# Moving fetches, stores, last sums and value products in a top-k attention and MLP kernel

## The chip, the cores and the metric

The kernel runs on one NeuronCore of a Trainium2 chip. A core has a matrix engine (PE, whose weight loads the profile lists apart as PEld), a vector engine (DVE), a scalar engine (ACT), a general engine (POOL) and a sync engine (SP). Each works through its own list of instructions, and semaphores tie them together. Nearly all DMAs of this kernel are issued by SP. The metric is the time of one execution on the device in microseconds (us); less is better.

## The reference

The inputs are `q`, `k`, `v` of shape 8 x 8 x 576 x 64 (batch, heads, sequence, head size), a gain of 512 and two weight matrices of 512 x 2048 and 2048 x 512. Attention keeps the 32 largest scores of each row, and an MLP with layer norm and a residual follows:

```python
scores = scale * np.matmul(q, k.transpose(0, 1, 3, 2))
kth = np.partition(scores, -32, axis=-1)[..., -32:-31]
scores = np.where(scores >= kth, scores, -1e9)
attn = np.exp(scores - scores.max(-1, keepdims=True))
attn = attn / (attn.sum(-1, keepdims=True) + 1e-9)
x = np.matmul(attn, v)                      # then heads side by side: 8 x 576 x 512
xn = (x - mean) / np.sqrt(var + 1e-6) * g_ln
out = x + np.maximum(xn @ w_ch1, 0.0) @ w_ch2
```

## The kernel before

**Units, jobs, groups.** A job is a pair of heads of one batch with some blocks of 128 queries; a unit is one query block of a job (both heads), or the last 64 rows of the sequence for both heads together (a rest unit). There are 160 units in 68 jobs of one to three units; the units of a job form a group. For each pair of heads the first job is fresh: `k` and `q` are loaded from the input (`load`, L316), turned by DVE (`turn_heads`, L343), and the turned `k` and late part of `q` are kept in DRAM (`keep_heads`, L357). Later jobs of the same pair are twins and read what was kept (`fetch_heads`, L364). The turned tiles (`kT`, `late_qT`) have two buffers each.

**The loop.** One loop runs over 166 steps, and the order in which it gives out instructions is the order on every engine. In step n: PE makes the scores of unit n+2 (unit n+1 up to step 16) in `scores` (L413), and ACT copies them out of PSUM (L394). DVE searches the 32nd largest value of unit n in four parts (`select`, L449 to L463) and starts unit n+1 (`halve`, L434), with POOL making the smaller halves (`lo`, L439 and L442). ACT masks unit n-1 (L490) and takes the exponentials of unit n-2 (L500). The exponentials of unit n-2 are turned to get keys on partitions, by PE and ACT copies (`turn`) or, for units that are not the last of their group in later batches, by DVE and two rounds of DMA (`move`, L532, L537, L540). The group that ended with unit n-3 gets its value products, 18 matmuls into `av` (`values`, L608 and L615), which ACT copies to `oT` (L620); PE turns them (L647) and ACT scales them into rows `x` (`place`, L624).

**Fill.** The MLP works on blocks of two row tiles. Its matmuls (`hidden` L748, `project` L905) wait in a list, and `fill`, called eight times a step, puts some of them between the other work, as many as a plan by costs allows. Each call advances a counter, `tick`. After the first block the projection uses seven products instead of eight: POOL makes sums of the hidden values (`sums` L835 to L837, `last_sum` L841), and differences of weights are made once in four steps (`form_pair`, L958 to L961), stored in DRAM (L963) and fetched for each block (L970).

**Later.** Work that needs not be done at once is held by `Later` lists and given out when it is old enough: `sums_later.settle(SUM_AGE)` with 7 ticks, once a step behind `halve` (L1226); `ends_later` with 6 ticks at each `fill`. A block's end is its scaling (ACT, L726), its residual (POOL, L721) and the stores of its rows (SP, L723). The residual puts the stores on a list, `stores`, and the next step's start sends them. `close` runs what is left of the previous block's ends when a block's projection begins.

**Plans.** `fetches` says in which step a twin's kept heads are fetched: `step = min(before.first, made - 1)`, where `made` is the step in which the job's first scores are made and `before.first` the first unit of the job before it. `fetch_heads` is called behind `halve` and `settle` of that step (L1229). The value products are called at L1213, behind two `fill`s. PSUM has five buffers for scores, turned tiles and `av`, and three for the MLP's products.

Of the kernel before, what the change touches and what calls it, by code (L numbers as in the profile page):

```python
# [29 lines left out]
def kernel(  # L30
# [41 lines left out]
    nc = tc.nc  # L72
# [174 lines left out]


    todo = []
    stores = []  # L250
    share = [0.0]
    owed = [0.0]

# [9 lines left out]
    tick = [0]  # L263

    class Later:
# [2 lines left out]
        def __init__(self):  # L268
            self.waiting = []

        def add(self, run):
            left = [run]

            def once():
                if left:
                    left.pop()()

            self.waiting.append((tick[0], once))
            return once

        def settle(self, age):
# [2 lines left out]
            for _, run in due_now:  # L284
                run()

    sums_later, ends_later = Later(), Later()

    def fill(least=0):
        tick[0] += 1  # L290
# [312 lines left out]
    def values(g):  # L603
        vb = g.job.v
        av = brief("av")
        for c in range(J):
            for h in range(2):
                nc.tensor.matmul(  # L608
                    av[h * D : (h + 1) * D, 0 : g.nq],
                    vb[:, h * J + c, :],  # L610
                    g.blocks[:, h, 0 : g.nq // 32, c, :],
                    start=(c == 0),
                    stop=False,
                )
        nc.tensor.matmul(  # L615
            av[:, 0 : g.nq], g.job.ends[:], g.pt[:, 2 * J, 0 : g.nq],
            start=False, stop=True,
        )
        g.oT = otpool.tile([P, GQ], FP32, tag="oT", name="oT")
        nc.scalar.copy(g.oT[:, 0 : g.nq], av[:, 0 : g.nq])  # L620

    def put(dst, ps, c0, den, d0):
        for h in range(2):
# [35 lines left out]
    class Block:  # L659
# [57 lines left out]
        def finish(self, i):  # L717
            o = self.o[i]

            def residual():  # L720
                nc.gpsimd.tensor_tensor(o[:], o[:], self.x[i], ALU.add)  # L721
                for dst, rows in self.dsts[i]:
                    stores.append(lambda d=dst, s=o[rows, :]: nc.sync.dma_start(d, s))  # L723

            def scaled():
                nc.scalar.activation(  # L726
                    o[:], o[:], AF.Identity,
                    bias=self.mv[:, i, 0:1], scale=self.rstd[:, i : i + 1],
                )
                self.ends.append(sums_later.add(residual))  # L730

            self.ends.append(ends_later.add(scaled))
# [83 lines left out]
        def seven(self):  # L816
# [47 lines left out]
            def evacuate(k):  # L864
# [4 lines left out]
                if k in home:  # L869
                    nc.scalar.copy(quarter(*home[k]), src)  # L870
                    if k == 1:
                        for j in range(G):
                            waiting[j]()
                            waiting[j] = sums_later.add(lambda j=j: last_sum(j))
                    return
                if k == 6:
                    joined[2]()
# [53 lines left out]
            )  # L931

    PER_ROW = 1.71e-3
    SUM_AGE, END_AGE, FETCH_AGE = 7, 6, 10
    blocks = []
    plain_done, formed, used, fetched = [None], [None], [], [0]

# [9 lines left out]
    def form_pair(i):  # L947

        lo, hi = slice(2 * i, 2 * i + 2), slice(NF // 2 + 2 * i, NF // 2 + 2 * i + 2)
        b11, b12 = w2[:, lo, 0 : 2 * P], w2[:, lo, 2 * P : DM]
        b21, b22 = w2[:, hi, 0 : 2 * P], w2[:, hi, 2 * P : DM]
        tt = nc.gpsimd.tensor_tensor
        x = xpool.tile([P, 2, DM], FP32, tag="x", name="form")
        t1, t2 = wt[:, 0, lo], wt[:, 1, lo]
        t4, t3 = (x[:, s].rearrange("p (f n) -> p f n", f=2) for s in range(2))
        tt(t1, b12, b11, ALU.subtract)  # L958
        tt(t2, b22, t1, ALU.subtract)
        tt(t3, t2, b11, ALU.subtract)  # L960
        tt(t4, b21, t2, ALU.subtract)  # L961
        for s in range(2):
            nc.sync.dma_start(scratch[:, s, i], x[:, s])  # L963
        if i == 3:
            formed[0] = now[0]
# [122 lines left out]
    for j in jobs[1:]:  # L1088
# [1 line left out]
        made = next(n for n in range(N) if units[j.first] in due(n))  # L1090
        step = min(before.first, made - 1)
        if j.twin:
            fetches.setdefault(step, []).append(j)
        else:
            turns[step] = j
            keeps[step + 1] = j
# [44 lines left out]
        return max(0.0, even) / SLOTS  # L1141

    recips, rows_of = {}, {}
    pairs_left = list(range(4))

    def arrived(n, key, x):
        blk, i = block_of[key]
# [18 lines left out]
    for n in range(END):  # L1166
# [16 lines left out]
        quick = ex.group if last and ex.group.quick else None  # L1183

        moved = ex is not None and ex.moved
        sent, stores[:] = stores[:], []

        if ex and not early:
            weigh(ex, 0)
        for x in due(n):  # L1190
            scores(x)
        if u:
            select(u, 0)
        for store in sent:
            store()
        if n in keeps:
            keep_heads(keeps[n])
        if n == gives_first:
# [12 lines left out]
            weigh(ex, 1)  # L1211
        fill()
        if g:  # L1213
            values(g)
        if parts and not moved:
            parts[0]()
        if ex and ex.rest:
# [8 lines left out]
        sums_later.settle(SUM_AGE)  # L1226
        for den in recips.pop(n, []):
            nc.vector.reciprocal(den, den)
        for j in fetches.get(n, []):  # L1229
            fetch_heads(j)  # L1230
        if n in turns:
            turn_heads(turns[n])
            later = fresh.index(turns[n]) + 1
# [37 lines left out]
        if quick:  # L1271

            values(quick)
            for den in recips.pop(n + 1):
                nc.vector.reciprocal(den, den)
            place(quick)
# [8 lines left out]
        for x in (g, quick):  # L1285
            if x and x.job.hp == NHP - 1:
                for qt in x.qts:
                    if qt < J:
                        arrived(n, (x.job.b, qt), xs[x.job.b, qt])
        if plain_done[0] is not None and plain_done[0] < n and len(pairs_left):  # L1290
            form_pair(pairs_left.pop(0))
        if late and late.job.hp == NHP - 1:
            r = late.job.b // 2
            if r % 2:
                for x in (r - 1, r):
                    arrived(n, ("r", x), rs[x])
        fill()
    while todo or stores or sums_later.waiting or ends_later.waiting:
        for store in stores:
            store()  # L1300
        stores.clear()
        tick[0] += 1
        ends_later.settle(1)
        sums_later.settle(1)
        fetch_forms(1)
# [33 lines left out]
```

## Time and profile before

| What | us |
|---|---|
| median of 3 runs | 1657.49 |
| range of the runs | 1655.69 to 1658.88 |
| the profiled execution | 1654.96 |
| its span, first to last instruction | 1653.2 |
| PE, DVE, ACT, POOL busy in it | 1513.9, 1459.4, 1069.8, 963.5 |
| PE's granted clock, mean | 0.968 |
| DVE's idle time at its costliest waits: scores' copies, exponentials' turns, row statistics | 14.8, 25.5, 21.8 |

The profile is of one execution. It lists busy time by engine and by groups of like instructions, who waited for whom, the chain of work that ended last, and the instructions in order of time. In a line such as `PE scps L413 <- DMA late_qT<-kept` the engine, the tile it writes and the line of code wait for what stands on the right. A line of the timeline gives start, duration, engine, line, operation, tiles (out<-in), shapes and count, and in brackets the idle time before it and what ended it. `PEld` is the weight load, `SPq` an issue on SP.

### The profile page before, as it was taken

The page shows a single profiled execution, that of the slowest core. Times are in us where ns is not written, and L with a number is a line of the kernel's source. Part 1 is how long each engine was busy: PE and PEld are TensorE (multiplying, and loading weights), DVE is VectorE, ACT ScalarE, POOL GpSimd, SP SyncE. Part 2 cuts the span into 40 slices and gives each one's busy share as a digit, 9 for nine tenths or more (in the row PEclk, how much of TensorE's full clock was granted, in tenths as well). Part 3 has the DMA queues.
Part 4 walks back from the last instruction along what each step waited for, and adds up shares of the span by engine and source line. Part 5 has one row for each costly group of instructions (what it writes and reads, how often), then busy time and mean ns, then how long its engine had stood idle before and what let it go on. Part 6 is the DMA issues. An engine that isn't in the chain of part 4 may idle for free.

```text
span 1653.2 us, 27838 instructions
## 1 busy us (share of the span) xinstructions
PE 1513.9 (92%) x7897; PEld 1128.3 (68%) x7897; DVE 1459.4 (88%) x4652; ACT 1069.8 (65%) x2712; POOL 963.5 (58%) x1492
## 2 busy tenths in 40 slices
PE   3668898899988998989999999999999999989998
PEld 1336556677665776767777776777767777768887
DVE  5999798999999999999999999999999999994000
ACT  6887776687755765757566766677656766654411
POOL 4778759656465455656565656564656565655243
PEclk9779899899998998999999999999999999999999
DMA  8533344312554455545655456535564545542211
GB/s 200 128 113 121 106 97 122 103 52 60 147 149 132 128 146 137 168 111 134 176 154 158 121 135 169 170 109 136 152 189 128 144 130 157 154 127 82 72 51 51
DMA packets 358945, 211.46 MB, mean 128 GB/s; under 512 B 250756, under 2 KB 331144, under 8 KB 358792
## 3 DMA queue, kind: packets, MB, share of 16 engines
q1 hardware_dynamic: 354056, 209.10, 45.1%
q10 hardware_dynamic: 4736, 0.59, 0.3%
q8 instruction: 63, 1.03, 0.3%
q14 instruction: 90, 0.74, 0.2%
HBM read 145.62 MB, written 63.96 MB: 127 GB/s over the span
## 4 chain that ended last, share of the span: by engine, by line
DVE 59%; PE 25%; POOL 7%; ACT 3%; DMA 2%; issue 2%; SPq 1%; DVEq 0%; ACTq 0%; POOLq 0%
DVE m L463 18%; DVE hi L449 15%; DVE hi L454 9%; PE ops L905 9%; PE hps L748 8%; DVE lo L449 5%; DVE sc L532 4%; DVE hi L434 4%; PE scps L413 3%; PE av L608 2%; POOL lo L442 1%; POOL lo L439 1%; DVE kT L343 1%; DVE st L675 1%; DMA late_qT<-kept 1%
## 5 line engine op out<-in xcount | busy, mean ns | idle before, releaser
L748 PE MATMUL hps<-xT,w 128*128 128x256 f32 x2304 | 557.3, 386 | 1.9 <-ACT xT L712 1.9
L463 DVE MAX8 m<-hi 128x8 f32<-128x304 f32 x1152 | 489.6, 462 | 3.3
L748 PEld LDWEIGHTS hps<-xT,w 128*128 128x128 f32 x2304 | 421.8, 192 | 81.5 <-issue 26.0
L439 POOL TENSOR_TENSOR lo<-sc,hi 128x576 int32<-128x576 int32 (+1 forms) x159 | 205.2, 1290 | 426.5 <-DVE hi L434 202.5
L449 DVE MATCH_REPLACE8 hi<-m,hi 128x304 f32<-128x304 f32 x864 | 391.2, 460 | 0.0
L905 PE MATMUL ops<-w,h 128*128 128x256 f32 x1360 | 332.1, 386 | 14.5 <-POOL h L841 14.5
L905 PEld LDWEIGHTS ops<-w,h 128*128 128x128 f32 x1360 | 248.3, 192 | 62.3 <-POOL h L841 16.9
L394 ACT COPY sc<-scps 128x288 f32<-128x288 f32 x576 | 197.9, 407 | 72.1 <-PE scps L413 52.4
L454 DVE MAX8 hi<-lo 128x8 f32<-128x288 f32 x576 | 234.3, 444 | 8.3 <-POOL lo L442 7.1
L500 ACT ACTIVATE e<-e,bias 128x576 f32<-128x576 f32 x288 | 225.0, 781 | 7.5 <-POOL bias L485 7.0
L490 ACT ACTIVATE e<-sc,m 128x576 f32<-128x576 f32 x288 | 224.4, 780 | 6.2 <-DVE sc L532 3.0
L442 POOL TENSOR_TENSOR lo<-lo,sc 128x576 int32<-128x576 int32 (+1 forms) x159 | 204.7, 1287 | 12.5
L413 PE MATMUL scps<-kT,late_qT 64*128 64x288 f32 (+3 forms) x832 | 127.6, 419 | 39.6 <-DMA late_qT<-kept 33.7
L608 PE MATMUL av<-pt,vb 128*64 128x256 f32 (+2 forms) x1088 | 150.1, 420 | 13.5 <-DMA pt<-turned 7.6
L413 PEld LDWEIGHTS scps<-kT,late_qT 64*128 64x128 f32 (+1 forms) x832 | 73.3, 171 | 91.6 <-issue 31.4
L771 ACT ACTIVATE h<-hps 128x512 f32<-128x512 f32 x144 | 86.4, 600 | 73.1 <-PE hps L748 72.3
L905 PE MATMUL ops<-wt,s 128*128 128x256 f32 x544 | 132.7, 384 | 0.0
L608 PEld LDWEIGHTS av<-pt,vb 128*64 128x64 f32 x1088 | 75.8, 144 | 80.0 <-issue 23.9
L620 ACT COPY oT<-av 128x256 f32<-128x256 f32 (+2 forms) x68 | 26.2, 385 | 154.5 <-PE av L615 154.0
L449 DVE MATCH_REPLACE8 lo<-hi,lo 128x288 f32<-128x288 f32 x288 | 125.7, 444 | 0.0
L434 DVE TENSOR_TENSOR hi<-sc 128x576 f32<-128x576 f32 (+1 forms) x160 | 111.1, 694 | 14.8 <-ACT sc L394 14.8
L532 DVE STREAM_TRANSPOSE sc<-e 128x512 f32<-128x512 f32 x144 | 93.3, 684 | 25.7 <-ACT e L500 25.5
(96 smaller groups left out, 1935.1 us busy)
## 6 DMA issues: line engine op xcount, KB each, us to landing
turned<-sc SPq DMA_DIRECT2D x72, 512.0 KB, 2.6
pt<-turned SPq DMA_DIRECT2D x288, 128.0 KB, 2.9
w<-forms SPq DMA_DIRECT2D x136, 256.0 KB, 4.0
vb<-in_v_dram SPq DMA_DIRECT2D x136, 128.0 KB, 3.4
raw<-in_moe_w_ch_dram SPq DMA_DIRECT2D x32, 512.0 KB, 4.3
kT<-kept SPq DMA_DIRECT2D x36, 288.0 KB, 3.6
kin<-in_k_dram SPq DMA_DIRECT2D x128, 72.0 KB, 2.5
kept<-kT SPq DMA_DIRECT2D x32, 288.0 KB, 3.1
```

The costliest lines, as they stand in the source:

```text
L394: nc.scalar.copy(u.sc[:, t, s * HALF : (s + 1) * HALF], made[s][t][:, 0:HALF])
L413: nc.tensor.matmul(ps[i * R : i * R + ql, o : o + width], qT[r, q0 : q0 + ql], kT[r, k0 : k0 + width], start=True, stop=True,)
L439: nc.gpsimd.tensor_tensor(lo.bitcast(I32), a.bitcast(I32), hi.bitcast(I32), ALU.subtract)
L442: nc.gpsimd.tensor_tensor(lo.bitcast(I32), lo.bitcast(I32), b.bitcast(I32), ALU.add)
L449: nc.vector.match_replace(x[:, t], m[:, t, :], x[:, t], LOWEST)
L454: nc.vector.max(u.hi[:, t, o : o + 8], u.lo[:, t])
L463: nc.vector.max(m[:, t, :], u.hi[:, t])
L490: nc.scalar.activation(u.e[:, t], u.sc[:, t], AF.Prelu, bias=u.thr[:, t, 7:8], scale=-1.0, alpha=SLOPE)
L500: nc.scalar.activation(u.e[:, t], u.e[:, t], AF.Exp, bias=u.bias[:, t : t + 1], scale=-scale / SLOPE, accum_out=g.den[:, col : col + 1],)
L608: nc.tensor.matmul(av[h * D : (h + 1) * D, 0 : g.nq], vb[:, h * J + c, :], g.blocks[:, h, 0 : g.nq // 32, c, :], start=(c == 0), stop=False,)
L748: nc.tensor.matmul(ps[0][:, side * N : (side + 1) * N], w1[:, c, f * P : (f + 1) * P], self.xT[:, c, 0:N], start=(c == 0), stop=(c == NC - 1),
L905: nc.tensor.matmul(bank[name][:, 0:Q], a(j), rhs, start=first and j == 0, stop=(j == G - 1), skip_group_check=not first,)
```

## The change

Six things change; none changes what is computed.

- A twin's kept heads are fetched in the step before the former one, and at another place in it: right behind the scores, the value products and the first part of `select`, ahead of stores and `keep_heads`.
- The value products (`values`) come directly behind the scores of the step. Their copy to `oT` becomes a function of its own, `take_values`, at the former place behind two `fill`s.
- The stores become a third `Later` list, given out at 8 ticks or more, once a step; each is also put on the block's ends, so that `close` gives it out.
- A last sum is entered as if it were 5 ticks older, so that it is due after 2.
- The stores of a pair of weight forms are given out a step after the pair is made (`keep_pair`).
- The closing loop gives out stores at an age of 2.

```diff
-    stores = []
-        def add(self, run):
+        def add(self, run, head_start=0):
-            self.waiting.append((tick[0], once))
+            self.waiting.append((tick[0] - head_start, once))
-    sums_later, ends_later = Later(), Later()
+    sums_later, ends_later, stores = Later(), Later(), Later()
@@ values
+        g.av = av
+
+    def take_values(g):
         g.oT = otpool.tile([P, GQ], FP32, tag="oT", name="oT")
-        nc.scalar.copy(g.oT[:, 0 : g.nq], av[:, 0 : g.nq])
+        nc.scalar.copy(g.oT[:, 0 : g.nq], g.av[:, 0 : g.nq])
@@ finish
-                    stores.append(lambda d=dst, s=o[rows, :]: nc.sync.dma_start(d, s))
+                    self.ends.append(
+                        stores.add(lambda d=dst, s=o[rows, :]: nc.sync.dma_start(d, s))
+                    )
@@ evacuate
-                            waiting[j] = sums_later.add(lambda j=j: last_sum(j))
+                            waiting[j] = sums_later.add(lambda j=j: last_sum(j), 5)
@@ ages
-    SUM_AGE, END_AGE, FETCH_AGE = 7, 6, 10
+    SUM_AGE, END_AGE, FETCH_AGE, STORE_AGE = 7, 6, 10, 8
@@ form_pair
+        return i, x
+
+    def keep_pair(made):
+        i, x = made
         for s in range(2):
             nc.sync.dma_start(scratch[:, s, i], x[:, s])
@@ the plan of fetches
-            fetches.setdefault(step, []).append(j)
+            fetches.setdefault(max(step - 1, 0), []).append(j)
@@ the step
-        sent, stores[:] = stores[:], []
         for x in due(n):
             scores(x)
+        if g:
+            values(g)
         if u:
             select(u, 0)
-        for store in sent:
-            store()
+        for j in fetches.get(n, []):
+            fetch_heads(j)
+        stores.settle(STORE_AGE)
...
         fill()
         if g:
-            values(g)
+            take_values(g)
...
-        for j in fetches.get(n, []):
-            fetch_heads(j)
...
-        if plain_done[0] is not None and plain_done[0] < n and len(pairs_left):
-            form_pair(pairs_left.pop(0))
+        if plain_done[0] is not None and plain_done[0] < n:
+            if made_pair:
+                keep_pair(made_pair.pop())
+            if pairs_left:
+                made_pair.append(form_pair(pairs_left.pop(0)))
@@ the closing loop
-    while todo or stores or sums_later.waiting or ends_later.waiting:
-        for store in stores:
-            store()
-        stores.clear()
+    while todo or any(x.waiting for x in (sums_later, ends_later, stores)):
         tick[0] += 1
+        stores.settle(2)
```

More of the change, by code (lines that the diff above doesn't have):

```diff
@@ L1143 @@
     recips, rows_of = {}, {}
-    pairs_left = list(range(4))
+    pairs_left, made_pair = list(range(4)), []
     def arrived(n, key, x):
@@ L1273 @@
             values(quick)
+            take_values(quick)
             for den in recips.pop(n + 1):
```

## The prediction

> **What bounds the kernel now.** I read the page's busy times and slices first, then busy time in stretches of 50 us, the waits by engine, the chain that ended last from 1430 us on, and the timeline where these point.
>
> ```profile
> PE 1513.9 (92%) x7897; PEld 1128.3 (68%) x7897; DVE 1459.4 (88%) x4652; ACT 1069.8 (65%) x2712; POOL 963.5 (58%) x1492
> ...
> PE   3668898899988998989999999999999999989998
> ...
> DVE  5999798999999999999999999999999999994000
> ```
>
> Three stages: DVE full and PE not (to about 1050 us), both full (to about 1450), then PE alone. Stretches (width; PE, PEld, DVE, ACT, POOL busy and counts; PE clock; DMA):
>
> ```profile
> 150.00:200.00 50.00, 42.92 (x190) 27.16 (x189) 41.55 (x138) 39.44 (x92) 39.25 (x36) 0.90 0.36 112
> 600.00:650.00 50.00, 40.41 (x211) 29.58 (x210) 48.18 (x150) 25.57 (x70) 27.45 (x47) 0.90 0.53 147
> 1400.00:1450.00 50.00, 48.25 (x250) 36.92 (x246) 49.59 (x158) 33.10 (x89) 32.21 (x53) 1.00 0.54 164
> 1500.00:1550.00 50.00, 50.00 (x259) 42.23 (x258) 11.94 (x36) 20.98 (x51) 24.81 (x52) 1.00 0.33 101
> ```
>
> From 405 to 1492 us DVE has one gap over 0.25 us in the trace, 1.20 us at 641. So a PE stall there costs nothing unless DVE stalls with it. Between 130 and 405 us DVE has 20.9 us of such gaps. From 1470 on PE has none over 0.15 us before its last matmul ends at 1646.3.
>
> ```profile
> ACT oT L620 <- PE av L615: 154.0, 59, 7.7
> PE scps L413 <- DMA late_qT<-kept: 33.7, 9, 12.1
> PE ops L905 <- POOL h L841: 14.5, 5, 7.8
> PE av L608 <- DMA pt<-turned: 7.6, 2, 5.8
> ```
>
> These waits (total us, times, longest) are what the change aims at. The timeline says which of them DVE or the end feels:
>
> ```profile
> 190.81 2.19 PE L413 MATMUL scps<-kT,late_qT 64*64 64x288 f32 x10 [3.82 <-DMA late_qT<-kept]
> 193.46 0.46 DVE L434 TENSOR_TENSOR hi<-sc 128x288 f32<-128x288 f32 x1 [2.31 <-ACT sc L394]
> 337.37 0.69 DVE L675 BATCH_NORM_STATS2 st<-x 128x6 f32<-128x512 f32 x1 [0.89 <-ACT x L624]
> 632.59 3.78 PE L905 MATMUL ops<-w,h 128*128 128x256 f32 x8 [7.80 <-POOL h L841]
> 641.95 0.71 DVE L532 STREAM_TRANSPOSE sc<-e 128x512 f32<-128x512 f32 x1 [1.20 <-ACT e L500]
> 1451.60 1.24 PE L413 MATMUL scps<-kT,late_qT 64*128 64x288 f32 x8 [3.24 <-DMA late_qT<-kept]
> ```
>
> The end of the chain leaves DVE and ACT at 1470 and is PE from there on:
>
> ```profile
> 1469.86 0.30 ACT sc L394
> 1470.16 0.14 issue
> 1470.30 0.63 PE tp L709 x4
> 1470.92 2.59 PE ops L905 x12
> ```
>
> [...]SP stood 343.0 us before L537 for DVE's transposes, and fetches stand behind these. [...]the 288 KB kT fetch[...]; the trace has a median of 3.6 us, which I use. [...]after a wait of 5.83 us the 18 value products at 478.79 took 5.75 us, against 3.11 at 503.31.
>
> **The change, part by part.** The profiled execution took 1654.96 us with a span of 1653.2; the median of the runs is 1657.49, 2.53 above. I sum on the profiled one and add 2.53.
>
> *Fetch one step sooner.* It issues the same two DMAs (SP about 0.45 us each), now ahead of stores, keeps, weight fetches and form fetches of that step, which come about 0.9 us later. The fetch for 1451.60 was issued at 1447.10, behind a transfer that waited for DVE until 1439.94. A step earlier it lies right behind the transfers that end at 1434.6, so lands near 1438.5, ten us before it is needed. A kT buffer must be free (two exist). For most jobs its last reader's scores were given out a step earlier. For the one-unit jobs near 190 us the last of four fetches will wait for scores of the next step; it did so already (SP waited 8.88 us until 202.79), and nothing but that step's loads is behind it. Gain at 190.81: PE was free at 187.0 and such scores take 1.20 us (as at 201.55), so they end at 188.2; ACT gets to their copies at 189.1, where its exponential ends, and two copies take 0.9: done at 190.0, before DVE is free at 191.15. So DVE's 2.31 us go: **-2.3**. The other fetch stalls (12.07 us at 283, 6.88 at 523, 3.48 at 711) ended in no DVE gap: 0.
>
> *Last sums.* Eight POOL sums of 0.457 us (3.4 us together) for each block, put at the first settling point at least 2 ticks after the flush, instead of 7; there is one point in a step of 8 ticks, behind the `lo` pair of the next unit. So they run up to a step sooner. The 7.80 us at 632.59 held ACT's exponential and with it DVE 1.20 us: **-1.2**. The 1.85 us at 1377.9 goes into the end, below. If POOL had no room, the bias pair L484/L485 would be 3.4 us late; POOL is at 58%, and its next use is a step away: 0.
>
> *Value products behind the scores.* 18 matmuls (2.6 to 3.1 us) move ahead of two fills, commonly 1.0 to 1.85 us of PE. Their copy stays where it was, so ACT, which waited 154.0 us for them, waits less. At 332.61 they started 0.99 us after the scores; the chain from there to `x` and the DVE statistics had 0.89 of gap: **-0.9**. The price: they now meet their own inputs. From each product's start, the end of the scores before it and the landing of its last transfer, 12 groups have a landing after the scores: by 7.18 us at 471, 4.80 at 1001, 3.01 at 604, 2.84 at 1215, 2.08 at 1160, the others 0.16 to 1.32. There PE stands, and the fill that covered the wait comes after it. DVE is full there and PE ahead of it, so 0, but it counts at the end. A 5.83 us stall at 473 gave no DVE gap, one of 7.80 gave 1.20; the 7.18 at 471 may give up to 0.6.
>
> *Stores and forms.* The output stores (40 DMAs) go a step later, which spares SP waits for POOL (95.4 us in 11 waits) off the path. If an output tile were needed sooner, ACT would wait: 0.8 us in all now, bounds 0 and +2; I take 0. Form pairs' 8 DMAs leave a step later, so six matmuls (2.3 us) at 305.85 wait a step: bounds 0 and 2.3, DVE is full there, 0.
>
> *The end.* PE relative to DVE from the products at 1218.59 on: their transfers landed at 1218.13, and 1.49 us of fill now follow, so PE is 1.0 later. At 1370 another 0.3. The last sums give back 1.85. At 1397 +0.7, at 1423 +0.2: PE is 0.4 late at 1448. The 3.24 go: 2.85 early. The next fetch stall (0.55 at 1466.8) goes too. The next products have transfers landed at 1466.31 and can start then; before, from the end of the scores at 1469.07 to the end of the products at 1480.34 lay 11.27 us, 0.64 of it a wait. New end 1466.31 + 10.63 = 1476.94: **-3.4**. After that PE had no wait, so this reaches the end. The 6.9 us after the last matmul stay.
>
> Sum: 2.3 + 1.2 + 0.9 + 3.4 = 7.8. 1654.96 - 7.8 = 1647.2; with 2.53, **1649.7 us**.
>
> **Rivals.** *The waits form again:* the ACT/POOL weight conversion at 200 us (DVE waits of 0.50 and 1.84 at 203 and 209) eats the 2.3, and PE at 1466 stands for the rows that POOL centres until 1467.9 or for ACT. Gain 0.5 + 1.2 = 1.7: about 1656. For it: PE's waits near 1466 and 1470 are short and DVE is near. Against: value products fill just that time.
>
> *Slower, the products at the head stall PE:* after 1150 PE has no spare time. Six groups (1160 to 1425) have landings after the scores. If each loses its fill of 1.5 us for good, 9.0 us, and the end's gain is lost, with 4.4 from DVE kept: 1657.49 - 4.4 + 9.0 = 1662.1. It is slower once more than 7.7 us are lost past 1150. For it: the negative slack. Against: a stalled PE is one that is ahead, and where PE lags (1238 to 1345) transfers landed 1.1 to 5.5 us before.
>
> *Not what it says:* if the fetch still landed late, held on SP behind another wait, only the sums and products would stay: 1657.49 - 2.1 = 1655.4. Against: SP's order above.
>
> **How the numbers follow.** Forecast (3.6 to 11 us faster, its own range 1646.5 to 1653.9) 0.50; still faster, since PE also loses small waits on ACT's `oT` (17.1 us of weight loads), 0.05; the two rivals near no change 0.25; slower 0.20. Under 0.2% (3.3 us) a measurement of this kernel can't tell from no change. Range 1644.5 to 1661.0.
>
> **What will show it.** Right: the waits of scores on `late_qT` nearly gone, those on `h L841` gone, ACT's on `av` cut by a third or more, DVE gaps at 191 and 641 gone, PE's final unbroken run starting about 7 us sooner. Wrong: DVE gaps over 0.5 us between 404 and 1492, more wait of L608 on transfers with PE's run after 1217 broken, POOL's `lo` late for L454, or SP standing at L364.

## The result, and the profile after

The changed kernel takes 1651.34 us, the median of 11 runs (1647.94 to 1655.99); the kernel before, run beside it, 1656.24 (1654.29 to 1658.88, 11 runs). The ratio is 0.9968 with a 95% interval of 0.9957 to 0.9979: faster by 5.3 us, 3.5 to 7.1. The forecast was 1649.7 us, 7.8 below the 1657.49 that it started from. All ratios in this document are of fast runs; one run of `x_stores`, of 5271.87 us, is left out of its ratio. The profiled execution took 1652.03 us, its span is 1650.0 us and PE's mean clock 0.959.

From here on line numbers are those of the kernel shown: the changed one has scores at L412, their copy at L393, the exponential at L499, DVE's turn at L531, value products at L607 and L614, their copy at L622, the MLP's first product (`hidden`) at L752 with its relu at L775, the second (`project`) at L909.

The page of the changed kernel, busy times and slices:

```profile
PE 1504.6 (91%) x7897; PEld 1134.6 (69%) x7897; DVE 1458.2 (88%) x4652; ACT 1064.0 (64%) x2712; POOL 958.4 (58%) x1492
...
PE   3569998999888988999999998999989999999998
...
DVE  5999898999999999999999999999999999994000
```

The stages are the same three. The stretches with the same columns as in the prediction (width; PE, PEld, DVE, ACT, POOL busy and counts; PE clock; DMA):

```profile
150.00:200.00 50.00, 45.96 (x227) 28.28 (x226) 43.06 (x142) 42.32 (x101) 40.59 (x38) 1.00 0.37 114
600.00:650.00 50.00, 47.37 (x248) 36.23 (x249) 49.38 (x150) 28.93 (x80) 25.10 (x45) 0.94 0.60 156
1400.00:1450.00 50.00, 50.00 (x265) 38.09 (x266) 49.66 (x161) 34.33 (x93) 33.98 (x61) 1.00 0.56 168
```

PE fills 47.4 of 50 us after 600, where it filled 40.4, and 50.0 after 1400, where it filled 48.3. The waits that answer to those shown of before (total us, times, longest):

```profile
ACT oT L622 <- PE av L614: 60.1, 28, 7.8
ACT h L775 <- PE hps L752: 115.3, 79, 9.1
PE av L607 <- DMA pt<-turned: 24.5, 11, 6.8
```

ACT's wait for `av` fell from 154.0 to 60.1 us; no wait of scores on `late_qT` is left (33.7 before), and 1.7 us of the projection's on `h` L845 (14.5 before). Two waits grew: value products on their transfers, 7.6 to 24.5 us (PE's idle time ahead of them, whatever the profile names as its end, 13.5 to 47.2), and ACT's relu on the MLP's first product, from 72.3 us to 115.3. The timeline, DVE and PE where the prediction pointed:

```profile
198.91 0.46 DVE L433 TENSOR_TENSOR hi<-sc 128x288 f32<-128x288 f32 x1 [0.25 <-ACT sc L393]
330.39 0.69 DVE L677 BATCH_NORM_STATS2 st<-x 128x6 f32<-128x512 f32 x1
470.89 4.54 PE L607 MATMUL av<-pt,vb 128*64 128x320 f32 x16 [6.76 <-DMA pt<-turned]
478.32 0.71 DVE L531 STREAM_TRANSPOSE sc<-e 128x512 f32<-128x512 f32 x1 [1.76 <-ACT e L499]
1227.50 0.71 DVE L531 STREAM_TRANSPOSE sc<-e 128x512 f32<-128x512 f32 x1 [1.63 <-ACT e L499]
1461.05 0.66 PE L553 MATMUL tp<-ident,e 128*128 128x128 f32 x4 [1.55 <-ACT e L499]
```

DVE's gaps near 191 us (2.31), 337 (0.89) and 641 (1.20) are gone, and the 1.84 at 209 has become 0.25. But where DVE had one gap over 0.25 us between 405 and 1480 us, it now has five, 5.67 us in all, each ahead of the turn of an exponential. And at 1461 PE stands for ACT, which it did not before. The chain that ended last:

```profile
1458.19 0.39 DVE m L462
1458.66 1.31 ACT sc L393 x4
...
1460.24 0.76 ACT e L499 x2
...
1462.84 1.80 PE scps L412 x4
1464.64 3.61 PE av L607 x16
```

DVE and ACT set the pace up to 1462.8 us, then PE alone. The 16 value products take 3.61 us there, at a clock of 0.50 (1463 to 1469 us); at 1303.89 us, at a clock of 1.00, such a group of 256 rows takes 1.95.

### The profile page after: what moved, and what is told of

The parts are those of the page before. It is cut to its first block, busy times and chain, and to the rows that moved or that the text cites. A ratio compares the mean times of both kernels' runs of the same rounds, so it can differ in the third digit from the quotient of the medians.

```text
span 1650.0 us, 27871 instructions
## 1 busy us (share of the span) xinstructions
PE 1504.6 (91%) x7897; PEld 1134.6 (69%) x7897; DVE 1458.2 (88%) x4652; ACT 1064.0 (64%) x2712; POOL 958.4 (58%) x1492
## 4 chain that ended last, share of the span: by engine, by line
DVE 65%; PE 19%; POOL 7%; ACT 3%; DMA 2%; issue 2%; SPq 1%; DVEq 0%; POOLq 0%; ACTq 0%
DVE m L462 19%; DVE hi L448 17%; DVE hi L453 10%; PE hps L752 8%; PE ops L909 6%; DVE lo L448 6%; DVE hi L433 5%; DVE sc L531 4%; PE av L607 2%; PE scps L412 1%; POOL lo L441 1%; POOL lo L438 1%; DVE st L677 1%; DVE kT L342 1%; POOL w L208 1%
## 5 line engine op out<-in xcount | busy, mean ns | idle before, releaser
L752 PE MATMUL hps<-xT,w 128*128 128x256 f32 x2304 | 547.5, 383 | 1.9 <-ACT xT L714 1.9
L752 PEld LDWEIGHTS hps<-xT,w 128*128 128x128 f32 x2304 | 422.0, 191 | 71.6 <-issue 15.4
L909 PE MATMUL ops<-w,h 128*128 128x256 f32 x1360 | 325.6, 383 | 1.7 <-POOL h L845 1.7
L909 PEld LDWEIGHTS ops<-w,h 128*128 128x128 f32 x1360 | 248.6, 191 | 42.9 <-issue 6.9
L393 ACT COPY sc<-scps 128x288 f32<-128x288 f32 x576 | 195.8, 409 | 58.2 <-PE scps L412 21.0
L499 ACT ACTIVATE e<-e,bias 128x576 f32<-128x576 f32 x288 | 225.5, 783 | 9.6 <-POOL bias L484 9.0
L607 PE MATMUL av<-pt,vb 128*64 128x256 f32 (+2 forms) x1088 | 158.1, 435 | 47.2 <-DMA pt<-turned 24.5
L607 PEld LDWEIGHTS av<-pt,vb 128*64 128x64 f32 x1088 | 81.6, 149 | 115.4 <-issue 42.2
L775 ACT ACTIVATE h<-hps 128x512 f32<-128x512 f32 x144 | 86.1, 598 | 115.8 <-PE hps L752 115.3
L412 PE MATMUL scps<-kT,late_qT 64*128 64x288 f32 (+3 forms) x832 | 128.7, 411 | 7.9 <-ACT pt L565 5.3
L909 PE MATMUL ops<-wt,s 128*128 128x256 f32 x544 | 129.2, 381 | 0.0
L531 DVE STREAM_TRANSPOSE sc<-e 128x512 f32<-128x512 f32 x144 | 93.8, 685 | 35.0 <-ACT e L499 34.9
L553 PE MATMUL tp<-ident,e 128*128 128x128 f32 x576 | 91.7, 284 | 29.9 <-ACT e L499 28.3
L412 PE MATMUL scps<-kT,qT 64*128 64x288 f32 x512 | 92.3, 461 | 27.9 <-DVE qT L342 26.1
```

Of the source, the lines that this page charges most:

```text
L393: nc.scalar.copy(u.sc[:, t, s * HALF : (s + 1) * HALF], made[s][t][:, 0:HALF])
L412: nc.tensor.matmul(ps[i * R : i * R + ql, o : o + width], qT[r, q0 : q0 + ql], kT[r, k0 : k0 + width], start=True, stop=True,)
L499: nc.scalar.activation(u.e[:, t], u.e[:, t], AF.Exp, bias=u.bias[:, t : t + 1], scale=-scale / SLOPE, accum_out=g.den[:, col : col + 1],)
L607: nc.tensor.matmul(av[h * D : (h + 1) * D, 0 : g.nq], vb[:, h * J + c, :], g.blocks[:, h, 0 : g.nq // 32, c, :], start=(c == 0), stop=False,)
L752: nc.tensor.matmul(ps[0][:, side * N : (side + 1) * N], w1[:, c, f * P : (f + 1) * P], self.xT[:, c, 0:N], start=(c == 0), stop=(c == NC - 1),
L909: nc.tensor.matmul(bank[name][:, 0:Q], a(j), rhs, start=first and j == 0, stop=(j == G - 1), skip_group_check=not first,)
```

## The experiments

Three theories stood at the start. A: the gain is DVE's and comes from the sooner fetch; products at the head of a step hold the fill behind them and with it ACT's exponentials, so they lose. B: the products gain, since they free ACT. C: the stores gain, by leaving SP free.

The table sums up all runs; the ratio is to the kernel before, run beside each. "Gaps" are DVE's idle times over 0.25 us in the profiled execution, in two stretches. "Mark" is the start of DVE's first operation (`halve`) on the eighth unit from the end, "end" that of PE's last matmul; both are taken from the traces. The last column, end minus mark, is what PE needs behind DVE's pace.

| Kernel | median us | ratio, 95% interval | gaps 185-405 | gaps 405-1480 | mark | end | end - mark |
|---|---|---|---|---|---|---|---|
| before | 1656.24 | 1 | 13.02 | 1.20 | 1425.5 | 1646.3 | 220.8 |
| after | 1651.34 | 0.9968 (0.9957-0.9979) | 7.66 | 5.67 | 1422.9 | 1643.1 | 220.2 |
| x_fetch | 1648.33 | 0.9951 (0.9939-0.9963) | 7.68 | 1.18 | 1418.9 | 1638.6 | 219.7 |
| x_fetch_first | 1653.53 | 0.9975 (0.9966-0.9984) | 9.25 | 1.63 | 1421.8 | 1645.3 | 223.5 |
| x_fetch_late | 1650.65 | 0.9970 (0.9959-0.9982) | 11.73 | 0.72 | 1422.7 | 1641.2 | 218.5 |
| x_values | 1664.28 | 1.0047 (1.0035-1.0059) | 12.91 | 10.20 | 1433.2 | 1653.7 | 220.5 |
| x_stores | 1655.27 | 0.9990 (0.9982-0.9997) | 11.87 | 0.35 | 1421.0 | 1641.6 | 220.6 |
| x_sums | 1657.64 | 1.0004 (0.9996-1.0012) | 14.28 | 1.15 | 1426.1 | 1650.0 | 223.9 |
| y_old_values | 1647.08 | 0.9943 (0.9930-0.9956) | 7.71 | 0.73 | 1418.3 | 1638.2 | 219.9 |
| z_early_values | 1648.04 | 0.9943 (0.9930-0.9955) | 7.73 | 1.13 | 1418.9 | 1639.3 | 220.4 |
| w_ready | 1644.17 | 0.9928 (0.9914-0.9942) | 7.74 | 0.53 | 1418.9 | 1634.9 | 216.0 |
| w_ready_old | 1646.95 | 0.9949 (0.9935-0.9962) | 7.67 | 0.00 | 1417.4 | 1638.0 | 220.6 |
| z_reserve | 1649.19 | 0.9960 (0.9948-0.9973) | 8.99 | 2.12 | 1422.0 | 1641.3 | 219.3 |
| z_centre | 1647.10 | 0.9947 (0.9935-0.9960) | 7.66 | 0.96 | 1418.5 | 1638.4 | 219.9 |

Gaps, mark and end are of one execution, and the ratios carry the verdicts: the trace of `x_stores`, for one, is of its fastest execution, 4.9 us under its median. The last column also holds PE's clock. Between 1440 and 1470 us it is halved (0.50 of full speed in the records) for 6.8 us in `after`, `x_fetch_first`, `x_sums`, `y_old_values`, `z_early_values` and `w_ready_old`, for 3.4 us in `x_fetch`, `x_values` and `z_centre`, and not at all in the other five. So the 223.5 and 223.9 of `x_fetch_first` and `x_sums` hold a halved stretch that the 220.8 of the kernel before does not; the last section comes back to it.

### The fetch alone

```diff
-            fetches.setdefault(step, []).append(j)
+            fetches.setdefault(max(step - 1, 0), []).append(j)
@@ the step: behind select(u, 0), no more behind halve
+        for j in fetches.get(n, []):
+            fetch_heads(j)
```

> The kernel before with kept heads fetched a step sooner and ahead of the stores, nothing else. Theory A (the gain is DVE's: its gaps of 2.31 us at 191 and of 0.50 and 1.84 us at 203 and 209 go because the scores come sooner): 4 to 5 us faster than before, DVE gaps at these places under 0.3 us, no score of PE waiting on late_qT after 200 us, and the 1.20 us gap at 641 still there. Rival B (the value products bring the gain, by freeing ACT): within 1.5 us of before. Rival C (the stores and form stores off SP bring it): within 1.5 us of before.

Measured: 1648.33 us, ratio 0.9951, so 8.1 us faster (6.1 to 10.1), more than the whole change and than A's 4 to 5 us. DVE loses 5.34 us less between 185 and 405 us: the 2.31 at 191, the 0.50 and 1.84 at 203 and 209 (0.26 is left of these), and the 0.89 at 337, which the prediction had put down to the value products. The stall of PE at 283 (12.07 us) is gone with it. So that stall did end in a DVE gap, 50 us later. The edit moves the fetch in two ways, a step sooner and ahead of the step's stores; no run separates them.

### The value products alone

```diff
         for x in due(n):
             scores(x)
+        if g:
+            values(g)
...
-            values(g)
+            take_values(g)
```

> The kernel before with the value products directly behind the scores and their copy where it was, nothing else. Theory A (products that wait at the head hold the fill and with it ACT's exponentials, and DVE's turns wait): 0 to 4 us slower than before, the 0.89 us gap at 337 gone, new DVE gaps of 0.7 to 1.8 us before the turned exponentials, 2 to 6 us in all between 405 and 1490. Rival B: 3 to 5 us faster than before. Rival C: within 1.5 us.

Measured: 1664.28 us, ratio 1.0047, 7.8 us slower (5.8 to 9.8), more than A's 0 to 4. B falls: ACT waits only 59.5 us for `av`, as after the whole change, and nothing is gained. DVE has eight gaps, 10.20 us in sum, between 405 and 1480 us, and its mark is 7.7 us later, which is the whole loss. The largest gap, in the timeline of this kernel (its relu is at L774, exponential L500, turn L532, projection L908, the copy of a projection L882):

```profile
637.42 1.24 PE L413 MATMUL scps<-kT,qT 64*128 64x288 f32 x8
638.59 2.37 PE L608 MATMUL av<-pt,vb 128*64 128x320 f32 x16
...
641.54 1.46 PE L908 MATMUL ops<-w,h 128*128 128x256 f32 x6
642.17 0.37 ACT L882 COPY t<-ops 128x256 f32<-128x256 f32 x1 [2.48 <-PE ops L908]
642.44 0.78 ACT L500 ACTIVATE e<-e,bias 128x576 f32<-128x576 f32 x1
643.34 0.71 DVE L532 STREAM_TRANSPOSE sc<-e 128x512 f32<-128x512 f32 x1 [3.53 <-ACT e L500]
```

Read upwards: DVE waits for an exponential; the exponential needs nothing from PE, but stands on ACT behind a copy of a projection (2.48 us idle ahead of it); and the projection stands on PE behind the value products. These wait for nothing here: PE is late from a stall for a last sum (5.54 us, until 631.65), and 3.1 us of products stand ahead of the fill.

### The whole change with the products at their old place

```diff
         for x in due(n):
             scores(x)
-        if g:
-            values(g)
...
         if g:
+            values(g)
             take_values(g)
```

> The changed kernel with the value products back behind two fills, all else as changed. Theory A: faster than the changed kernel by 2 to 6 us (1645 to 1649 us where before is 1656), no DVE gap over 0.5 us between 405 and 1490. Rival B: 3 to 5 us slower than the changed kernel. Rival C: the same as the changed kernel within 1.5 us.

Measured: 1647.08 us, ratio 0.9943: 4.1 us faster than the changed kernel by the two ratios, and the fastest, with `z_early_values` and `z_centre`, of the versions that do the whole computation. It beats both kernels; from the fetch alone (0.9951) it can't be told. DVE's gaps between 405 and 1480 us fall from 5.67 to 0.73. The timeline at the place where the changed kernel had its first gap, first with the products at the old place:

```profile
465.48 1.56 PE L752 MATMUL hps<-xT,w 128*128 128x256 f32 x6
471.59 4.53 PE L607 MATMUL av<-pt,vb 128*64 128x320 f32 x16 [4.55 <-DMA pt<-turned]
468.36 0.64 ACT L775 ACTIVATE h<-hps 128x512 f32<-128x512 f32 x1
468.85 0.81 ACT L499 ACTIVATE e<-e,bias 128x576 f32<-128x576 f32 x1
476.91 1.28 DVE L531 STREAM_TRANSPOSE sc<-e 128x512 f32<-128x512 f32 x2
```

and then the changed kernel:

```profile
476.30 1.89 PE L752 MATMUL hps<-xT,w 128*128 128x256 f32 x8
476.93 0.60 ACT L775 ACTIVATE h<-hps 128x512 f32<-128x512 f32 x1 [9.12 <-PE hps L752]
477.43 0.77 ACT L499 ACTIVATE e<-e,bias 128x576 f32<-128x576 f32 x1
```

PE stands for the same transfer in both, until 471. At the old place the fill has gone ahead at 465.48, its relu is done at 469.0, the exponential behind it at 469.7, and DVE turns both halves in one go (x2) without a gap. In the changed kernel the fill comes at 476.30, behind products that waited 6.76 us; the relu waited 9.12 us for it, the exponential came at 477.43, and DVE, idle for 1.76 us, turned the second half at 478.32. The exponential stands behind the relu in ACT's list: its input was long ready (its mask was done at 463.8), and it starts 0.50 us after the start of a relu that waited 9.12. This last link is read from the timelines: no run put the exponential ahead of the relu.

### Stores and form stores alone

```diff
-        sent, stores[:] = stores[:], []
...
-        for store in sent:
-            store()
+        stores.settle(STORE_AGE)
@@ after the pair is made
+            if made_pair:
+                keep_pair(made_pair.pop())
```

> The kernel before with output stores and form stores given out a step later (and the stores in close), nothing else. Theory A: within 1.5 us of before, though SP's waits for POOL before stores fall from 95 to under 50 us. Rival B: within 1.5 us. Rival C: 3 to 5 us faster than before.

Measured: 1655.27 us, ratio 0.9990: 1.7 us faster (0.5 to 3.0). Its waits, in the trace of its fastest execution, suggest why it isn't nothing: scores wait 21.5 us for `late_qT` in place of 33.7 (longest 6.4 in place of 12.1), and SP stands for POOL's output rows 78.0 us in place of 95.4 (A had under 50). The stores that waited on SP had stood ahead of fetches; the stall at 283 and the DVE gap at 337 go here too. So stores and fetch take part of the same loss away.

### The last sums alone

```diff
-                            waiting[j] = sums_later.add(lambda j=j: last_sum(j))
+                            waiting[j] = sums_later.add(lambda j=j: last_sum(j), 5)
```

> The kernel before with the last sums of the feed-forward given out at the younger age alone. Prediction: the PE wait on h of 7.80 us at 632 goes and with it DVE's gap of 1.20 at 641, and PE's 1.85 us at 1378: 1 to 3 us faster, 1654.5 to 1656.5 us. Rival (POOL and DVE meet elsewhere: sums ahead of the lo pair or the bias pair make these late): no faster, 1657 to 1659 us, with new DVE gaps of select behind lo.

Measured: 1657.64 us, ratio 1.0004: no gain. PE waits 2.5 us for `h`, not 14.5, and the gap of 1.20 at 641 is gone. In its place stand 1.50 us at 337 (0.89 before) and three gaps of 0.26 to 0.48 after 1050. The expectation of 1 to 3 us misses; the rival's time holds, though not by its mechanism: no new gap of `select` behind `lo` appears.

### The fetch in two halves

```diff
+            sooner = j.b == 0
+            if sooner:
+                firsts.setdefault(max(step - 1, 0), []).append(j)
+            else:
+                fetches.setdefault(step, []).append(j)
@@ the step: behind select(u, 0)
+        for j in firsts.get(n, []):
+            fetch_heads(j)
```

This is `x_fetch_first`, on the kernel before; `x_fetch_late` has `j.b > 0` there.

> The kernel before with the fetch of kept heads moved forward for the jobs of the first batch alone; all later fetches stay where they were. Theory A (the fetch pays where DVE has gaps, early; the rest at the end): the DVE gaps at 191 us (2.31) and at 203 and 209 us (0.50 and 1.84 to about 0.25) go, the stall of 12.07 us at 283 and the gap of 0.89 at 337 stay, and so does PE's wait of 3.24 us near 1448: 4 to 5 us faster than before, about 1653 us. Rival (the end is what pays, since PE sets it): under 1.5 us faster, since the fetches near 1450 are as late as before. If it is as fast as the version with all fetches moved (8 us faster), the later fetches are worth nothing.

> The kernel before with the fetch of kept heads moved forward for all jobs but those of the first batch. The version with all moved was 8 us faster than before, the one with the first batch alone 4. Theory A (the parts add): 3.5 to 5 us faster than before, about 1653 us; DVE's gaps of 2.31, 0.50 and 1.84 at 191 to 209 us stay, the 0.89 at 337 goes, and PE's wait of 3.24 us near 1448 goes. Rival (they don't add; early gains reach the end only if the late fetches are in time): under 1.5 us faster. By the prediction's own split (0.9 at 337 and 3.4 at the end): 4.3 us faster.

Measured: 4.1 us (2.7 to 5.6) for the first batch, 5.0 us (3.0 to 6.8) for the later ones, and the product of the ratios, 0.9945, is that of all fetches, 0.9951: within these intervals the halves add. The early one takes 3.77 us of DVE's gaps between 185 and 405 us. The late one keeps most of these, takes the gap at 337, and brings the end 2.3 us nearer to the mark than in the kernel before, the clock being whole in both (1.00 from 1440 to 1475 us); PE's wait of 3.24 us at 1451 is gone:

```profile
1445.41 1.24 PE L413 MATMUL scps<-kT,late_qT 64*128 64x288 f32 x8
...
1462.34 1.23 PE L413 MATMUL scps<-kT,late_qT 64*128 64x288 f32 x4 [0.33 <-ACT r L624]
1464.28 0.66 PE L709 MATMUL tp<-ident,x 128*128 128x128 f32 x4 [0.72 <-POOL x L684]
```

This is the timeline of `x_fetch_late`. What comes in its place are short waits for ACT and for the rows that POOL centres.

### Are the products slow because they wait, or because they come first?

```diff
                     vb[:, h * J + c, :],
-                    g.blocks[:, h, 0 : g.nq // 32, c, :],
+                    w1[:, c, h * 512 : h * 512 + g.nq]
+                    if g.units[0].moved
+                    else g.blocks[:, h, 0 : g.nq // 32, c, :],
```

`w_ready` has this with the products ahead, as in the changed kernel, `w_ready_old` with the products behind two fills. Both leave the attention weights of those groups out of the output.

> The kernel after, but the value products of groups with units that DVE turns read w1 (resident) in place of the turned weights, so that they need no transferred tile: this leaves the attention weights of those groups out of the output; transposes and transfers still run, only the products don't stand for them. Theory A (products at the head stand for their transfers, and the fill, the relu and the exponential behind them are late): PE's waits of value products on transfers go, the DVE gaps before turned exponentials between 405 and 1490 us fall from 5.7 to under 1.5 us, and the time is 1645 to 1649 us, 2 to 6 us below the kernel after. Rival A2 (it is the mere order: 2.6 to 3.1 us of products ahead of the fill delay hidden, relu and exponential whether they wait or not): gaps stay near 4 to 6 us and the time at 1650 to 1653 us.

> The kernel after with the value products back behind the step's two fills, and those of groups with units that DVE turns reading w1 in place of the turned weights (this leaves the attention weights of these groups out of the output): the fourth corner of place of the products against readiness of their tiles. So far: products ahead and waiting 1651.3 us, behind the fills and waiting 1647.1, ahead and ready 1644.2. Theory A (only ahead and waiting costs; mere order costs nothing): 1644 to 1647 us, so that the place of the products makes under 1.5 us when their tiles are ready. Theory A3 (tiles ready, the products ahead even gain, since they fill PE's wait for rows near 1458 us): 1646 to 1648 us, 2 to 3 us slower than ahead and ready. Rival A2 (order costs by itself): under 1643 us.

Measured: with tiles that are ready, products ahead give 1644.17 us (0.9928), products behind 1646.95 (0.9949). So the place of the products is worth 4.1 us against them when they wait for transfers, and some 3.5 us for them when they don't (these two intervals just overlap). Reading `w1` by itself is worth nothing: `w_ready_old` takes what `y_old_values` takes, 1647.08. A2, that mere order costs whether the products wait or not, falls; A3 fits. In `w_ready` the same step reads (here the relu is at L777, the `hidden` product at L754):

```profile
466.83 2.59 PE L607 MATMUL av<-w,vb 128*64 128x320 f32 x16
...
469.99 1.89 PE L754 MATMUL hps<-xT,w 128*128 128x256 f32 x8
470.62 0.60 ACT L777 ACTIVATE h<-hps 128x512 f32<-128x512 f32 x1 [0.63 <-PE hps L754]
471.12 0.77 ACT L499 ACTIVATE e<-e,bias 128x576 f32<-128x576 f32 x1
477.83 1.29 DVE L531 STREAM_TRANSPOSE sc<-e 128x512 f32<-128x512 f32 x2
```

The products run directly behind the scores, the relu waits 0.63 us in place of 9.12, and the turn has no gap. Two things come out of it. DVE's mark is 1418.9 against 1417.4 with the products behind: coming first costs DVE 1.5 us even so, if two profiled executions can be set against each other that closely. And PE's end is 4.6 us nearer to the mark. Of this, 1.3 us are waits: PE stands for 1.99 us in place of 1.30 and 2.02, since ready products fill the wait for rows. Some 2.6 us are the clock, which is whole here (1.00 from 1440 to 1475 us): 8 turns of rows and 12 projections take 1.32 and 2.75 us, and 2.06 and 4.56 in `w_ready_old`, whose clock is 0.76 and 0.56 in the two stretches of 5 us from 1455 on. That the prediction's step for the end is right is seen here once the transfers are out of the way; how much of the 3.5 us is owed to a clock that happened to stay whole is open.

Order is not free everywhere. The changed kernel's gap at 687 us stands behind products that waited for nothing:

```profile
681.17 1.24 PE L412 MATMUL scps<-kT,late_qT 64*128 64x288 f32 x8
682.34 2.37 PE L607 MATMUL av<-pt,vb 128*64 128x320 f32 x16
...
686.35 0.60 ACT L775 ACTIVATE h<-hps 128x512 f32<-128x512 f32 x1 [2.90 <-PE hps L752]
687.73 0.71 DVE L531 STREAM_TRANSPOSE sc<-e 128x512 f32<-128x512 f32 x1 [0.77 <-ACT e L499]
```

PE makes these scores 1.8 us ahead of DVE's next `halve` (at 682.98); in `w_ready` it makes them 6.2 us ahead, and there the same order costs no gap. So a wait seems to cost twice: where it stands, and by the lead that PE lacks in later steps.

### Products ahead only where no transfer is late

```diff
+        ahead = n < jobs[5 * NHP].first + 3
-        if g:
+        if g and ahead:
             values(g)
...
+            if not ahead:
+                values(g)
```

> The kernel after with the value products behind the scores only as long as no group has units turned by DVE with late transfers (batch 0 and the steps up to the first such group of its later jobs), and behind two fills from there on. Theory A: as fast as the version with all products behind the fills (1647.1 us), within 2 us; the DVE gaps between 405 and 1490 us stay under 1.5 us in sum. Rival B (early products help where nothing is late, by freeing ACT sooner): 1 to 2 us faster than that version, 1645 to 1646 us. If it is slow as the kernel after (1651), the harm is done early, where transfers are not late, and Theory A falls.

Measured: 1648.04 us, ratio 0.9943, that of `y_old_values`. The harm is not in the early steps, as A has it; and early products bring nothing that can be told by themselves, against B.

### What limits the end?

The edit

```diff
-    RESERVE = 4.0
+    RESERVE = 9.0
```

is `z_reserve`, and

```diff
-            if now[0] <= gives_first:
+            if now[0] <= gives_first or now[0] >= 150:
```

is `z_centre`. Both are put on `y_old_values`, whose PE stands 1.30 and 1.45 us for the last rows near 1457 us.

> The kernel after with the value products back behind the fills and 9.0 in place of 4.0 us of filling work held back for the time before the next block of rows is given out. The question is what PE's two waits near 1457 us (1.30 and 1.45 us, for the last rows) and the halved clock behind them cost. Theory E (they take the gain at the end away): the waits go, the clock stays whole there, 2 to 5 us faster than the version without the larger reserve (1647.1 us). Rival (PE's waits there don't set the end, or the held work is missing earlier): 1646 to 1649 us, with new DVE gaps or PE waits before 1450 us.

> The kernel after with the value products back behind the fills and the rows that are ready from step 150 on (of 160) centred on DVE in place of POOL. Theory E (PE near 1457 us stands for POOL's centring, behind its lo): the wait of 1.45 us for rows goes, the clock is halved for less time or not at all, 1 to 4 us faster than the version with POOL (1647.1 us). Rival (DVE sets the end of its own work by then, and the rows wait for it): 1647 to 1649 us.

Measured: 1649.19 and 1647.10 us against 1647.08. Theory E falls as it was put. In `z_reserve` the waits are gone and the clock is whole (1.00 from 1440 to 1475 us), but DVE's wait for POOL at 292 us grew from 1.64 to 2.92, 2.12 us of gaps stand at 857 to 885, and its mark is 3.7 us later; from mark to end it gained 0.6. The filler was not to be had for nothing. In `z_centre` PE waits 1.45 us for the same rows, now from DVE: the rows are late whoever centres them. The clock is halved for 3.4 us in place of 6.8, as E has it (0.66 from 1460 to 1465 us; 0.68 and 0.63 from 1455 to 1465 in `y_old_values`), and the time is the same.

## Why the prediction was right, and where it was wrong

The time, 1651.34 us, lies 1.6 above the forecast of 1649.7 and inside its own range; the case that came true is the forecast's, faster by more than a measurement can tell from no change. But that the sum of 7.8 us came near 5.3 is luck: its errors cancel. Of its own signs, those of being right came (the waits, the gaps at 191 and 641, PE's last unbroken run 7.5 us sooner, from 1462.84), and so did two of being wrong: four DVE gaps over 0.5 us between 404 and 1480, and more waits of products, two of which (1.75 us at 1367, 1.15 at 1394) break PE's run after 1217. By its steps:

**Fetch one step sooner, -2.3: right in mechanism, too small.** The gap at 191 went as worked out. But the same jobs' next units also gained, 0.50 and 1.84 at 203 and 209, which the first rival had as what would eat the gain. The first batch's fetches alone measure 4.1 us.

**"The other fetch stalls ended in no DVE gap: 0": wrong.** The stall of 12.07 us at 283 ended in the gap of 0.89 at 337. Four of the fourteen traces have that stall (before, `x_values`, `x_fetch_first`, `x_sums`: 12.07, 12.19, 13.86, 13.74 us), and they have the gap (0.89, 0.60, 1.54, 1.50); the ten others have neither. The chain ran through rows and statistics, 50 us of it, and looking at the next DVE instruction after a stall missed it. So of the 0.9 that was ascribed to the products, nearly all was the fetch's: the products alone took the gap from 0.89 to 0.60.

**Last sums, -1.2: the gap went, the gain did not come.** 1.0004. Some 1.8 us of gaps appeared elsewhere (0.61 more at 337, behind a stall at 283 that is 1.67 us longer, and 1.15 after 1050). In company it may still matter: the 3.53 us gap of `x_values` stands behind a stall for a last sum (5.54 us at 631), the changed kernel has no such gap there, and the products cost 4.1 in it and 7.8 alone, a difference of 3.7. That is argued from traces; sums and products without the other parts were not run.

**Value products, -0.9 with a price of 0: the step that failed.** Measured: +7.8 alone, +4.1 in the changed kernel. The text saw the 12 groups whose transfers land after the scores, and the stalls came much as listed: 6.76, 5.17, 4.65, 2.72 and 1.62 us, where it had 7.18, 4.80, 3.01, 2.84 and 2.08. The failed sentence is "DVE is full there and PE ahead of it, so 0", with 0.6 at most for the 7.18 at 471, which came out as 1.76. PE was ahead of DVE, but not everything DVE waits for comes from PE directly. Fill that is held on PE holds its relu, or its copy, on ACT, and behind these in ACT's list stands the exponential of a unit that DVE turns (at 476.93 us a relu that waited 9.12, the exponential 0.50 us behind it). The bound from the stalls of before (5.83 us of stall and no gap at 473) was taken with the fill ahead of the stall, and so with the relu already fed; the change took just that cover away. What the stalls take from PE's lead seems to make later steps pay too, as at 687 us, where no product waits.

**Stores and forms, 0: small, but not nothing.** -1.7 us (0.5 to 3.0): they had stood ahead of fetches on SP, and the stall at 283 goes with them. The prediction had read in the trace that fetches stand behind SP's waits (343.0 us before L537), and did not apply it to the stores.

**The end, -3.4: mechanism right, size off.** From mark to end the changed kernel gained 0.6 us (220.8 to 220.2), `x_fetch_late` 2.3, `w_ready` 4.8, these two at the whole clock (1.00). Scores no longer waited for `late_qT`, products ran directly behind scores, as told. What was left out: PE, now early, runs into ACT and DVE, 1.55 us at 1459.5, and then its clock is halved. The stretches of the changed kernel there, with the columns as above (PE's clock is the third number from the end):

```profile
1455.00:1460.00 5.00, 4.44 (x24) 2.96 (x22) 5.00 (x17) 2.81 (x9) 0.19 (x1) 1.00 0.30 112
1460.00:1465.00 5.00, 3.61 (x15) 2.10 (x17) 4.93 (x18) 4.97 (x14) 4.15 (x6) 0.75 0.84 212
1465.00:1470.00 5.00, 5.00 (x25) 2.95 (x22) 5.00 (x17) 1.16 (x5) 0.76 (x3) 0.57 0.00 0
```

The products of that group took 4.83 us, 2.3 more than at the full clock (2.57 at 1477.77 us in the kernel before, clock 1.00). What such a stretch costs at the end can be read from two kernels that are alike there: `x_fetch_first` differs from the kernel before in the fetches of the first batch alone, and stands for `late_qT` near 1447 us as long (3.18 us against 3.24), but behind this its clock is halved for 6.8 us, the next 16 products take 2.8 us longer (last section), and its end lies 2.7 us further from the mark. 0.6 + 2.7 is 3.3 of the 3.4. These are single executions, and no run changed the clock alone: that the halved clock took the rest is argued, not shown.

Put together as measured: fetch -8.1, stores -1.7, sums +0.6 (not told from 0), products +4.1 in company: -5.1, against -5.3. That fetch and stores share the stall at 283 is not taken off in this sum, and the intervals, some 2 us to each side for the fetch, have room for it. Of the rivals, the slower one had the right event, products that stand at the head of a step, and the wrong place for its cost: not PE after 1150 us, but DVE through ACT's order, two thirds of its gaps before 1060 us. The other rivals fall: the fetches land in time, and the weight conversion ate nothing.

## What to carry to other kernels

When work that may stall is moved ahead in an engine's list, follow everything behind it one engine further: what its consumers hold up in their own lists counts, even if the engine that sets the pace needs nothing from the stalled one. A measured stall that cost nothing bounds the cost of another only if the same work went ahead of it. And a gap that a stall causes may lie 50 us away: to find out what a stall costs, follow its products to where the slowest engine meets them.

## What the runs showed of the hardware that was not expected

The matrix engine's clock was halved, to 0.50 of full speed, after short waits, and in these traces the length of a wait did not tell whether it would be. The longest gaps ahead of a halving were 1.55 us (changed kernel; clock 0.75 and 0.57 in the two stretches of 5 us from 1460 on), 1.30 (`y_old_values`; 0.68 and 0.63 from 1455 on) and two of 0.34 and 0.70 (`x_fetch`; 0.66 from 1460 to 1465); and in `w_ready` one gap of 1.99 us was followed by a full clock:

```profile
1455.00:1460.00 5.00, 3.01 (x22) 1.65 (x20) 4.93 (x16) 3.46 (x12) 3.30 (x4) 1.00 0.82 206
1460.00:1465.00 5.00, 4.94 (x29) 4.04 (x26) 5.00 (x18) 1.87 (x6) 1.64 (x5) 1.00 0.06 14
```

The wait for `late_qT` near 1450 us shows it best: 3.24 us in the kernel before, 3.18 in `x_fetch_first`. Behind it the same eight products of scores and eight of a projection follow, first in the kernel before, then in `x_fetch_first`:

```profile
1451.60 1.24 PE L413 MATMUL scps<-kT,late_qT 64*128 64x288 f32 x8 [3.24 <-DMA late_qT<-kept]
1452.77 1.99 PE L905 MATMUL ops<-wt,s 128*128 128x256 f32 x8
...
1447.74 2.29 PE L413 MATMUL scps<-kT,late_qT 64*128 64x288 f32 x8 [3.18 <-DMA late_qT<-kept]
1449.96 3.78 PE L905 MATMUL ops<-wt,s 128*128 128x256 f32 x8
```

They take 3.2 us with the whole clock (1.00) and 6.0 with the halved one. What decides between the two was not shown: no run changed such a wait alone.

The work behind the wait paid 2.3 us in the changed kernel; in `x_fetch` and `y_old_values`, 8 turns of rows took 2.07 us (1.32 in `w_ready`) and 12 projections 3.64 and 3.75 (2.75), some 1.7 us together.
